# A decode layer pair on one core: more of one pair's values rest in PSUM, and two query weights are loaded into other places

## The chip, the cores and the metric

The kernel runs on one core of a Trainium2 chip. The metric is the device time of one execution in microseconds (us), as a median of several runs. A 95% interval of a ratio is typically 0.13% wide to each side, which is 0.7 us here.

## The reference, cut to what matters

A decoder step for one token, twice over: attention on a cache of 4096 keys and values for each of 32 heads of 192, then a gated feed-forward block of 640 to 1536 to 640. Everything is bf16.

```
x = x + A(layernorm(x))       # q = x wq; softmax(q k^T / sqrt(192)) v; wo
x = x + B(layernorm(x))       # (sigmoid(x wg) * (x wu)) wd
x = x + A(layernorm(x))       # the same weights and the same cache again
x = x + B(layernorm(x))
```

One token means no reuse: each key and value byte enters one product per layer. Heads are handled in 16 pairs. One pair's keys with its Wq, or its values with its Wo, are 3.64 MB; all pairs together are 116 MB. On-chip memory holds seven such units and a smaller region, so the second layer loads nearly all of it again. What is kept from layer 0 to layer 1 is not loaded twice: pairs 0, 14 and 15, the keys of pair 1, and a part of the values of pair 1 in PSUM banks that are free at that time.

## The kernel before: the parts that matter

All loads go through one queue of SyncE, in the order of a list `seq`. A load is issued as soon as what it overwrites has been read, so **a load that must wait holds up every load behind it**. The list at the turn from layer 0 to layer 1 (`MW` are the feed-forward weights in three cuts, `MV` the values of pair 1 in the region where the feed-forward weights lie):

```python
NST = 3 * FW // 2                              # FW = 640
stash = [bank[i][:, 0:NST // 2].bitcast(U32) for i in (3, 6)]
...
MW = {"wg0": (0, 0, 3), ..., "d2": (11, 6, 9), "d3": (14, 9, 12)}     # first cell of the region, from, to
MV = {"v1": (17, len(rc)), "v0": (0, 6), "v2": (6, 11), "v3": (11, 14)}   # cells of FW columns
ST = MV["v3"][1] * FW
VAFTER = {"v0": "u3", "v1": "u1", "v2": "d1", "v3": "d3"}
...
seq += [("wol", 14), ("wol", 15)] + [(k,) for k in (*MW, *MV)] + [("a0", 0), ("wom",), ("a0", 1), ("a0", 2), ("a", 1, 3), ("b", 1, 2)]
...
elif k == "a0":                                # Wq, then keys of pair 2, in three loads
    if f"a14_{it[1]}" not in ev_done:          # over pair 14's Wq and keys: after its Q, after its QK
        return False
    s = A_SLOT[1][2]
    o0, o1 = ((0, WQE), (WQE, A0CUT), (A0CUT, UNIT))[it[1]]
    pg.dma(q_dma(slot(s, o0, o1 - o0), a_in(2, o0, o1)), ...)
```

`("a0", 0)` is the Wq of pair 2. It overwrites pair 14's Wq, so it cannot be issued before layer 1 has computed Q of pair 14 (its queries, the product of x with that Wq). `wom` is Wo of pair 1 (it overwrites pair 1's Wq, so it waits for Q of pair 1). Layer 1 begins with:

```python
mark("a14_0", Q(14, 0))
mark("QM", Q(PM, 1, 5))                        # PM = 1
for i in range(2):                             # values of pair 1: back from PSUM to SBUF
    pg.op("dve", lambda v, i=i: words(v, mreg(ST + i * NST, NST), stash[i]), ...)
ln_sq(xi)
mark("a14_1", QK(14, 0, ks=(0,)))
mark("a14_2", QK(14, 0, ks=(1, 2)))
...
soft(1)
expo(1)
QK(0, 0)
```

## Time and profile before

| | before |
|---|---|
| median of the first 3 runs | 515.14 us (514.93 to 515.77) |
| span of the profiled run | 513.6 us |
| loaded by queue q1 | 218.63 MB |

In the views PE is the matrix engine, PEld its weight loads, DVE VectorE, ACT ScalarE, POOL GpSimd, and SPq the issues of SyncE. The page of the kernel before: the span, busy time by engine, GB/s in 40 slices of 12.8 us, the load queue (packets, MB, share of the 16 DMA engines' span), and the chain that ended last by engine.

```profile
span 513.6 us, 8573 instructions
PE 263.4 (51%) x3716; PEld 137.6 (27%) x3716; DVE 99.2 (19%) x376; ACT 85.2 (17%) x171; POOL 4.2 (1%) x31
...
GB/s 430 425 422 425 426 429 439 451 443 425 429 425 434 426 443 451 435 425 429 411 416 417 410 438 435 433 425 427 453 443 434 434 429 429 426 430 423 426 427 276
...
q1 hardware_dynamic: 9512, 218.63, 99.1%
...
DMA 63%; PE 24%; DVE 7%; ACT 2%; SPq 2%; issue 2%; DVEq 0%; POOL 0%; ACTq 0%; POOLq 0%
```

No engine but the DMA is near its limit. The weakest slices, 20 to 23, are 244 to 295 us, the feed-forward block and the turn into layer 1.

The end of the chain in order of time (start, length, what): the last load lands at 486.16 + 24.89 = 511.05 us.

```profile
486.16 24.89 DMA big<-in_wd_dram
```

The windows view at the turn: window, its length, busy time (and instructions) of PE, PEld, DVE, ACT and POOL, the granted clock, the mean busy share of the DMA engines, GB/s.

```profile
288.00:290.00 2.00, 1.70 (x39) 1.23 (x42) 1.17 (x5) 0.00 (x0) 0.00 (x0) 0.50 1.02 420
290.00:292.00 2.00, 2.00 (x20) 0.55 (x13) 1.03 (x5) 0.00 (x0) 0.00 (x0) 0.50 1.02 406
292.00:294.00 2.00, 1.65 (x29) 1.28 (x29) 1.39 (x2) 0.44 (x2) 0.00 (x0) 0.50 0.96 367
294.00:296.00 2.00, 2.00 (x24) 0.49 (x12) 0.23 (x1) 0.42 (x2) 0.00 (x0) 0.50 1.08 437
```

From 292 to 294 us the stream moves 367 GB/s. The timeline around it: start, length, engine, line. The two SyncE lines are the issues of Wq of pair 2 and Wo of pair 1; line 166 is the copies back from PSUM.

```profile
288.91 0.33 SPq L212 DMA_DIRECT2D big<-in_uc_dram  x1
...
289.31 1.38 SPq L212 DMA_DIRECT2D big<-in_uc_dram  x1
...
289.49 1.34 DVE L166 TENSOR_SCALAR big<-bank 128x480 uint32<-128x480 uint32 x2
290.74 0.15 DVE L361 SCALAR_TENSOR_TENSOR sc<-bank,sc 128x5 f32<-128x5 f32 x1
```

**Measures taken from the packet records of the traces.** The trace has each DMA packet with its time and size; one packet is one row of one load.

- *Outstanding* at an issue: the bytes of all earlier loads minus the bytes moved so far, as time at 428 GB/s, the stream's mean.
- *Packet time* of a load: eight rows per engine, each 7.0 ns plus its size over 27.13 B/ns. This fits the median rows: 102 ns for 2560 B, 149 for 3840, 291 for 7680, 1053 for 28416. The fixed part agrees in kind with the Trainium skill, "DMA: Bandwidth & Descriptors", section "Why small descriptors are slow (HBM only)", which has a fixed overhead per packet.
- *The turn*: from the mark of the last down-projection load `d3` to the mark of pair 3's keys. The mark of a load is the moment when as many bytes have arrived as it and all loads before it hold. It is not the arrival of the load's own last row: the 16 DMA engines run unevenly, and in the kernel before the last row of `d3` came at 286.20 us, 1.1 us after its mark. *Beyond packet times* is the turn's length minus the packet times of its loads.

### The profile page before, as it was taken

To read this page: it belongs to the slowest core of one execution; us is meant where nothing else is said; L and a number is where in the kernel's file an instruction comes from. 1 tells how busy PE (TensorE), PEld (TensorE's weight loads), DVE (VectorE), ACT (ScalarE), POOL (GpSimd) and SP (SyncE) were. 2 spreads that over 40 slices of the span, in tenths; PEclk is the share of its full clock that TensorE was granted. 3 is DMA by queue.
4 is the path that set the end of the run, shared out by engine and by line. 5 is a ranking of instruction groups with operands and counts; after the bars stand their busy time and mean duration, and the time that the engine had idled before them with its cause. 6 is when DMAs were issued, how large, how long until landed. Compare 5 with 4: busy or idle time off the path is not lost.

```text
span 513.6 us, 8573 instructions
## 1 busy us (share of the span) xinstructions
PE 263.4 (51%) x3716; PEld 137.6 (27%) x3716; DVE 99.2 (19%) x376; ACT 85.2 (17%) x171; POOL 4.2 (1%) x31
## 2 busy tenths in 40 slices
PE   0462456344643265345566767864625245634665
PEld 0221222122311132222234434432312122212334
DVE  0221212112211121111121333231202112210311
ACT  0110111011110111011120033130301011101220
POOL 0010000000000000000000000000000000000000
PEclk9955665565566755566575568676857555556655
DMA  9999999999999999999999999999999999999996
GB/s 430 425 422 425 426 429 439 451 443 425 429 425 434 426 443 451 435 425 429 411 416 417 410 438 435 433 425 427 453 443 434 434 429 429 426 430 423 426 427 276
DMA packets 9676, 218.97 MB, mean 426 GB/s; under 512 B 1208, under 2 KB 1208, under 8 KB 4664
## 3 DMA queue, kind: packets, MB, share of 16 engines
q1 hardware_dynamic: 9512, 218.63, 99.1%
q8 instruction: 13, 0.21, 0.1%
q10 hardware_dynamic: 144, 0.06, 0.0%
q14 instruction: 7, 0.06, 0.0%
HBM read 218.69 MB, written 0.00 MB: 426 GB/s over the span
## 4 chain that ended last, share of the span: by engine, by line
DMA 63%; PE 24%; DVE 7%; ACT 2%; SPq 2%; issue 2%; DVEq 0%; POOL 0%; ACTq 0%; POOLq 0%
DMA big<-in_uc_dram 54%; PE scores L410 8%; PE o L467 7%; DMA big<-in_wd_dram 6%; DVE sc L420 3%; DMA big<-in_wu_dram 3%; PE bank L426 2%; SPq L212 2%; PE bank L395 2%; PE bank L502 1%; ACT e_sb L434 1%; PE bank L440 1%; ACT diag L423 1%; DVE sc L452 1%; DVE qs L398 1%
## 5 line engine op out<-in xcount | busy, mean ns | idle before, releaser
L410 PE MATMUL scores<-big,qs 128*32 128x512 bf16 x744 | 81.5, 605 | 9.9 <-DVE qs L398 9.9
L395 PE MATMUL bank<-sh,big 128*128 128x1 bf16 x465 | 17.1, 166 | 133.0 <-DMA big<-in_uc_dram 130.7
L467 PE MATMUL o<-big,et_sb 128*2 128x384 bf16 x1024 | 78.7, 474 | 5.9 <-DMA big<-in_uc_dram 3.4
L423 ACT ACTIVATE diag<-cst,sc 128x128 f32<-128x128 bf16 x32 | 12.8, 402 | 307.5 <-DVE sc L420 299.4
L420 DVE TENSOR_REDUCE sc<-scores 128x1 f32<-128x1024 f32 x31 | 38.0, 1225 | 79.2 <-PE scores L410 79.2
L395 PEld LDWEIGHTS bank<-sh,big 128*128 128x128 bf16 x465 | 14.6, 103 | 136.2 <-DMA big<-in_uc_dram 113.4
L426 PE MATMUL bank<-diag,sc 128*128 128x128 f32 x64 | 22.5, 447 | 47.9 <-ACT diag L423 47.9
L434 ACT ACTIVATE e_sb<-scores,sc 128x1024 bf16<-128x1024 f32 x31 | 37.4, 1205 | 41.8 <-DVE sc L429 39.5
L467 PEld LDWEIGHTS o<-big,et_sb 128*2 128x2 bf16 x1024 | 28.0, 108 | 43.8 <-issue 31.1
L398 DVE TENSOR_TENSOR qs<-bank,cst 128x96 bf16<-128x96 f32 x31 | 8.0, 258 | 162.4 <-PE bank L395 162.4
L410 PEld LDWEIGHTS scores<-big,qs 128*32 128x32 bf16 x744 | 23.7, 131 | 43.0 <-issue 29.6
L426 PEld LDWEIGHTS bank<-diag,sc 128*128 128x128 f32 x64 | 14.1, 274 | 73.0 <-ACT diag L423 71.5
L474 ACT CAST o_sb<-o 128x384 bf16<-128x384 f32 x64 | 29.8, 474 | 22.5 <-PE o L467 22.3
L502 PE MATMUL bank<-sh,big 128*128 128x1 bf16 x480 | 17.2, 165 | 15.2 <-DVE sh L491 14.6
L444 DVE CAST et_sb<-bank 128x64 bf16<-128x64 f32 x32 | 7.2, 225 | 71.8 <-PE bank L440 71.8
L502 PEld LDWEIGHTS bank<-sh,big 128*128 128x128 bf16 x480 | 14.5, 99 | 17.7 <-DVE sh L491 12.1
L427 DVE TENSOR_REDUCE sc<-bank 128x2 f32<-128x128 f32 x32 | 9.3, 292 | 42.1 <-PE bank L426 42.1
L440 PE MATMUL bank<-cst,e_sb 128*128 128x8 bf16 x256 | 11.7, 169 | 6.8 <-ACT e_sb L434 6.7
L440 PEld LDWEIGHTS bank<-cst,e_sb 128*128 128x128 bf16 x256 | 8.9, 101 | 22.9 <-issue 16.4
L450 PE MATMUL o<-sc 128*128 128x2 f32 x62 | 14.0, 295 | 0.6 <-ACT o_sb L474 0.6
L450 PEld LDWEIGHTS o<-sc 128*128 128x128 f32 x62 | 12.1, 243 | 1.9 <-ACT o_sb L474 1.3
L452 DVE RECIPROCAL sc<-o 64x1 f32<-64x1 f32 x62 | 10.2, 164 | 9.5 <-PE o L450 7.8
(76 smaller groups left out, 106.4 us busy)
## 6 DMA issues: line engine op xcount, KB each, us to landing
big<-in_uc_dram SPq DMA_DIRECT2D x20, 7104.0 KB, 22.6
big<-in_uc_dram SPq DMA_DIRECT2D x12, 3552.0 KB, 21.2
big<-in_uc_dram SPq DMA_DIRECT2D x1, 3072.0 KB, 21.5
big<-in_uc_dram SPq DMA_DIRECT2D x4, 768.0 KB, 11.6
big<-in_uc_dram SPq DMA_DIRECT2D x5, 480.0 KB, 6.9
big<-in_uc_dram SPq DMA_DIRECT2D x1, 2048.0 KB, 10.7
big<-in_uc_dram SPq DMA_DIRECT2D x1, 2016.0 KB, 10.6
big<-in_wg_dram SPq DMA_DIRECT2D x4, 480.0 KB, 14.7
```

The source lines that it names most:

```text
L395: ins = t.matmul(qe[:, i:i + 1], lhsT=slot(sa, c * 2 * DH + c0, P), rhs=xq[:, c:c + 1], start=(c == 0), stop=(c == DC - 1))
L410: ins = t.matmul(sc_x[1 + b][32 * j:32 * j + 32, :], lhsT=qs[:, y, k, :], rhs=slot(sa, WQE + k * W + (4 * b + j) * 512, 512), start=(k == ...
L420: pg.op("dve", lambda v: v.reduce_max(out=mx, in_=sc_x[0][:], axis=AX.X), wr=[res("mx")], ex=sc_x[3:5])
L423: pg.op("act", lambda a: a.mul(out=diag[:], in_=ident, mul=mx), rd=[res("cst"), res("mx")], wr=[res("diag")])
L426: pg.op("pe", lambda t: t.matmul(dmx[:, 0:P], lhsT=ones_f, rhs=diag[:], start=True, stop=True), rd=[res("diag"), res("ones")], ex=[rb[2]])
L434: pg.op("act", lambda a: a.activation(out=e_sb[:], in_=sc_x[0][:], func=ACT.Exp, bias=nbias, scale=srs_c, accum_out=rowsum), rd=[res("nbia ...
L440: ins = t.matmul(qe[:, 0:2 * NB].rearrange("p (r x) -> p r x", r=2)[:, :, 4 * b:4 * b + 4], lhsT=e_sb[:, b * P:(b + 1) * P], rhs=sel, star ...
L450: pg.op("pe", lambda t: t.matmul(sm, lhsT=ones_f, rhs=rs2[z], start=True, stop=True), rd=[res(f"rs2{z}"), res("ones")], wr=[res("rsum")], ...
L452: rb[bk].last["dve"] = pg.op("dve", lambda v, h=h: v.reciprocal(out=Rn[z][64 * h:64 * h + 64], in_=sm[64 * h:64 * h + 64, h:h + 1]), rd=[r ...
L467: ins = t.matmul(o8[h][32 * j:32 * j + 2, 0:2 * DH].rearrange("p (a d) -> p a d", a=2), lhsT=et_sb[:, z, h * NB + 2 * u:h * NB + 2 * u + 2 ...
L474: pg.op("act", lambda a, h=h: a.copy(out=o8_sb[:, :, h * DH:(h + 1) * DH], in_=o8[h][:, 0:2 * DH].rearrange("p (a d) -> p a d", a=2)), wr= ...
L502: ins = t.matmul(yT[:, j:j + 1], lhsT=wo[:, c * D + j * P:c * D + (j + 1) * P], rhs=oTb[z][:, c:c + 1], start=False, stop=(c == 2), skip_g ...
```

## The change

It has two parts. First, the third resting place: 507 more fp32 words of each partition, the unused part of bank 7, which else holds only the five columns of the output accumulator. That is 1014 more columns of pair 1's values that layer 1 need not load. Second, the order: the Wq of pair 2 goes into cells of pair 1's values (which must then come back from PSUM later, after that Wq has been used), and the Wq of pair 3 into the place of pair 14's Wq. So the load that must wait for Q of pair 14 is now the Wq of pair 3, and two loads that need not wait stand before it. Q of pair 2 is computed early, kept as three columns, and used when its turn comes.

```diff
-    stash = [bank[i][:, 0:NST // 2].bitcast(U32) for i in (3, 6)]
+    stash = [(bank[i][:, c:c + n].bitcast(U32), 2 * n) for i, c, n in ((3, 0, NST // 2), (6, 0, NST // 2), (7, DC, 512 - DC))]
+    NSV = sum(n for _, n in stash)
 ...
-    MV = {"v1": (17, len(rc)), "v0": (0, 6), "v2": (6, 11), "v3": (11, 14)}
+    MV = {"v1": (17, len(rc)), "v0": (NSV // FW, 6), "v2": (6, 11), "v3": (11, 14), "v4": (14, 17)}
+    VAFTER = {"v1": "u1", "v0": "d1", "v2": "u3", "v3": "d2", "v4": "d3"}
 ...
-    seq += [...] + [(k,) for k in (*MW, *MV)] + [("a0", 0), ("wom",), ("a0", 1), ("a0", 2), ("a", 1, 3), ("b", 1, 2)]
+    seq += [...] + [(k,) for k in (*MW, "v1", "wq2", "v0", "v2", "v3", "v4", "wq3", "wom")] + [("a0", 1), ("a0", 2), ("a", 1, 3), ("b", 1, 2)]
 ...
+        elif k == "wq2":                      # Wq of pair 2, over the first down-projection weights
+            if "done_d0" not in ev_done:
+                return False
+            pg.dma(q_dma(mreg(0, WQE), a_in(2, 0, WQE)), k, wr=rc[0:WQE // FW])
+        elif k == "wq3":                      # Wq of pair 3, over pair 14's
+            if "a14_0" not in ev_done:
+                return False
+            pg.dma(q_dma(slot(A_SLOT[1][2], 0, WQE), a_in(3, 0, WQE)), k, wr=[res(k)], extra=[ev_done["a14_0"]])
 ... # layer 0: a third copy into PSUM, behind the softmax of pair 2
+            if (l, prev) == (0, PM):
+                stow(2, [ev])
 ... # layer 1
             mark("QM", Q(PM, 1, 5))
-            for i in range(2):
-                pg.op("dve", lambda v, i=i: words(v, mreg(ST + i * NST, NST), stash[i]), ...)
             ln_sq(xi)
 ...
-            soft(1)
+            soft(1, hook=lambda: Q(2, None))
+            for i in (2, 0, 1):
+                o, n = sum(m for _, m in stash[:i]), stash[i][1]
+                pg.op("dve", lambda v, i=i, o=o, n=n: words(v, mreg(o, n), stash[i][0]), ..., ex=[rb[7]] if i == 2 else [], own="st")
             expo(1)
```

The loads of the turn, in queue order, with the bytes of one row:

```
before: v1 2816 | v0 7680 | v2 6400 | v3 3840 | Wq2* 3840 | Wo1* 3840 | keys2* 8192, 16384 | Wq3+keys3* 28416
after:  v1 2816 | Wq2 3840 | v0 1812 | v2 6400 | v3 3840 | v4 3840 | Wq3* 3840 | Wo1* 3840 | keys2* 8192, 16384 | keys3* 24576
(* waits for PE's work of layer 1)
```

More of the change, by code (lines that the diff above doesn't have):

```diff
@@ L51, in __init__, with op @@
         self.seg = None
-    def op(self, eng, fn, rd=(), wr=(), ex=(), multi=False, own=None):
+    def op(self, eng, fn, rd=(), wr=(), ex=(), multi=False, own=None, after=()):
         d = {}
@@ L70, in op @@
                     add(ev)
+        for ev in after:
+            add(ev)
         if eng == "pe":
@@ L129, in decode_kernel @@
     et_sb = sb("et_sb", [P, 2, 2 * NB], BF16)
-    sc = sb("sc", [P, 27 + 5 * DC + 2 * FC], FP32)
+    sc = sb("sc", [P, 30 + 5 * DC + 2 * FC], FP32)
+    q2 = sc[:, 27 + 5 * DC + 2 * FC:30 + 5 * DC + 2 * FC]
     tick = sc[0:1, 24 + 5 * DC + 2 * FC:25 + 5 * DC + 2 * FC]
@@ L181, in decode_kernel @@
     MAFTER = {"d0": ("wg0",), "d1": ("wg1",), "u2": ("wg2",), "u3": ("wg3",), "d2": ("wg3", "u0"), "d3": ("u1",)}
-    MV = {"v1": (17, len(rc)), "v0": (0, 6), "v2": (6, 11), "v3": (11, 14)}
-    VAFTER = {"v1": "u1", "v0": "d1", "v2": "u3", "v3": "d2"}
-    ST = MV["v3"][1] * FW
-    VAFTER = {"v0": "u3", "v1": "u1", "v2": "d1", "v3": "d3"}
+    MV = {"v1": (17, len(rc)), "v0": (NSV // FW, 6), "v2": (6, 11), "v3": (11, 14), "v4": (14, 17)}
+    VAFTER = {"v1": "u1", "v0": "d1", "v2": "u3", "v3": "d2", "v4": "d3"}
     PLACE = {s: i for i, s in enumerate((0, 3, 2, 1, 4, 5, 6))}
@@ L227, in decode_kernel @@
     seq = [("a", 0, 0)] + [("c", 0, p) for p in range(1, 15)] + [("a", 0, 15), ("b", 0, 14)] + last_values(0, 15)
-    seq += [("wol", 14), ("wol", 15)] + [(k,) for k in (*MW, *MV)] + [("a0", 0), ("wom",), ("a0", 1), ("a0", 2), ("a", 1, 3), ("b", 1, 2)]
+    seq += [("wol", 14), ("wol", 15)] + [(k,) for k in (*MW, "v1", "wq2", "v0", "v2", "v3", "v4", "wq3", "wom")] + [("a0", 1), ("a0", 2), ("a", 1, 3), ("b", 1, 2)]
     seq += [("b", 1, 3), ("a", 1, 4), ("b", 1, 4), ("a", 1, 5), ("a", 1, 6), ("b", 1, 5)]
@@ L265, in try_load @@
                 return False
-            pg.dma(q_dma(slot(s, 0, UNIT), a_in(it[2])), f"c{it[1]}{it[2] % 2}" if it[1:] in ((0, 15), (1, 4), (1, 5), (1, 6), (1, 13)) else f"a{it[1]}_{it[2]}", wr=[rslot[s]])
+            o0 = WQE if it[1:] == (1, 3) else 0
+            pg.dma(q_dma(slot(s, o0, UNIT - o0), a_in(it[2], o0)), f"c{it[1]}{it[2] % 2}" if it[1:] in ((0, 15), (1, 4), (1, 5), (1, 6), (1, 13)) else f"a{it[1]}_{it[2]}", wr=[rslot[s]])
         elif k == "b":
@@ L290, in try_load @@
             s = A_SLOT[1][2]
-            o0, o1 = ((0, WQE), (WQE, A0CUT), (A0CUT, UNIT))[it[1]]
+            o0, o1 = ((WQE, A0CUT), (A0CUT, UNIT))[it[1] - 1]
             pg.dma(q_dma(slot(s, o0, o1 - o0), a_in(2, o0, o1)), f"a0{it[1]}", wr=[res(f"a0{it[1]}")] + ([rslot[s]] if it[1] == 2 else []),
@@ L307, in try_load @@
             c0, c1 = MV[k]
-            o0, o1 = c0 * FW, min(c1 * FW, ME)
+            o0, o1 = max(c0 * FW, NSV), min(c1 * FW, ME)
             pg.dma(q_dma(mreg(o0, o1 - o0), b_in(PM, o0, o1)), k, wr=rc[c0:-(-o1 // FW)])
+        elif k == "wq2":
[6 more added lines that the diff above has]
+            pg.dma(q_dma(slot(A_SLOT[1][2], 0, WQE), a_in(3, 0, WQE)), k, wr=[res(k)], extra=[ev_done["a14_0"]])
         elif k == "wom":
@@ L390, in Q @@
             sa = A_SLOT[l][p]
+            w, rw = slot(sa, 0, WQE), [rslot[sa]]
+            if (l, p) == (1, 2):
+                w, rw = mreg(0, WQE), rc[0:WQE // FW]
+            elif (l, p) == (1, 3):
+                s2 = A_SLOT[l][2]
+                w, rw = slot(s2, 0, WQE), [rslot[s2], res("wq3")]
             def f(t):
@@ L394, in f @@
                     for c in range(DC):
-                        ins = t.matmul(qe[:, i:i + 1], lhsT=slot(sa, c * 2 * DH + c0, P), rhs=xq[:, c:c + 1], start=(c == 0), stop=(c == DC - 1))
+                        ins = t.matmul(qe[:, i:i + 1], lhsT=w[:, c * 2 * DH + c0:c * 2 * DH + c0 + P], rhs=xq[:, c:c + 1], start=(c == 0), stop=(c == DC - 1))
                 return ins
-            ev = pg.op("pe", f, rd=[res("xq"), rslot[sa]] + ([res("a00")] if l == 1 and p == 2 else []), ex=[rb[bk]])
+            ev = pg.op("pe", f, rd=[res("xq")] + rw, ex=[rb[bk]])
+            if y is None:
+                pg.op("dve", lambda v: v.tensor_copy(out=q2, in_=qe[:, 0:3]), wr=[res("q2")], ex=[rb[bk]])
+                return ev
             pg.op("dve", lambda v: v.tensor_tensor(out=qs[:, y], in0=qe[:, 0:3].unsqueeze(2).to_broadcast([P, 3, 32]), in1=mask3, op=ALU.mult),
@@ L412, in f @@
                 return ins
-            ev = pg.op("pe", f, rd=[res(f"qs{y}"), rslot[sa]] + ([res("a00"), res("a01"), res("a02")] if l == 1 and p == 2 else []), ex=sc_x[3:5])
+            ev = pg.op("pe", f, rd=[res(f"qs{y}"), rslot[sa]] + ([res("a01"), res("a02")] if l == 1 and p == 2 else []), ex=sc_x[3:5])
             if ks[-1] == 2 and not (l == 0 and ("a", p) in KEPT) and not (l == 1 and p in (PM, 14)):
@@ L522, in PVn @@
                 release(sv)
+            return ev
         def scale_pm():
@@ L526, in scale_pm, with stow @@
                   rd=[res("cst"), res("srs")], wr=[res("pm_s")])
+        def stow(i, after=()):
+            sv, o = B_SLOT[0][PM], sum(n for _, n in stash[:i])
+            ev = pg.op("dve", lambda v: words(v, stash[i][0], slot(sv, v_at(PM) + o, stash[i][1])), rd=[rval[sv]], wr=[res(f"stash{i}")], own="st", after=after)
+            rslot[sv].rd.append(ev)
         def step(p, prev):
             if l == 0 and prev > 0:
-                PVn(prev - 1, 1 - prev % 2)
+                ev = PVn(prev - 1, 1 - prev % 2)
             Q(p, 0)
@@ L553, in loop @@
                     if (l, p) == (0, PM):
-                        sv = B_SLOT[0][PM]
-                        for i in range(2):
-                            ev = pg.op("dve", lambda v, i=i: words(v, stash[i], slot(sv, v_at(PM) + ST + i * NST, NST)), rd=[rval[sv]], wr=[res(f"stash{i}")], own="st")
-                            rslot[sv].rd.append(ev)
+                        stow(0)
+                        stow(1)
             pg.seg = None
@@ L577, in attention @@
             mark("QM", Q(PM, 1, 5))
-            for i in range(2):
-                pg.op("dve", lambda v, i=i: words(v, mreg(ST + i * NST, NST), stash[i]), rd=[res(f"stash{i}")], wr=rc[ST // FW:ST // FW + 3], own="st")
             ln_sq(xi)
@@ L589, in attention @@
             Q(0, 0)
-            soft(1)
+            soft(1, hook=lambda: Q(2, None))
+            for i in (2, 0, 1):
+                o, n = sum(m for _, m in stash[:i]), stash[i][1]
+                pg.op("dve", lambda v, i=i, o=o, n=n: words(v, mreg(o, n), stash[i][0]), rd=[res(f"stash{i}")], wr=rc[o // FW:-(-(o + n) // FW)],
+                      ex=[rb[7]] if i == 2 else [], own="st")
             expo(1)
@@ L604, in attention @@
             ET(1)
-            Q(2, 0)
+            pg.op("dve", lambda v: v.tensor_tensor(out=qs[:, 0], in0=q2.unsqueeze(2).to_broadcast([P, 3, 32]), in1=mask3, op=ALU.mult),
+                  rd=[res("cst"), res("q2")], wr=[res("qs0")])
             packed(2, 0, PM)
```

## The prediction

> **What bounds the kernel.** The load stream. The queue table gives q1 99.1% of the 16 DMA engines' span, 218.63 MB; the chain of waits is 63% DMA and ends in a weight load (486.16 to 511.09 us). PE is busy 51%, VectorE 19%. The last loads, from 482.9 us on, are issued far ahead (by the packet records 4 us of data is outstanding at the first, 22 us at the last), so the end moves with the stream, and compute counts only where it lets the stream run dry.
>
> Where does it? I added up, from the packet records, bytes issued minus bytes moved at each issue. The low point is the turn into layer 1, with small loads that wait for PE: 2.4 us is outstanding when the Wq of pair 2 is issued (288.91 us, after Q of pair 14). The next issue, Wo of pair 1, took 1.38 us instead of 0.33, while the two 0.65 us copies from PSUM ran on VectorE (289.5 to 290.8). In the windows view 292 to 294 us moves only 367 GB/s. The four loads from pair 2's Wq to its keys end about 0.6 us later than their packet times explain.
>
> **What changes, costed.**
> 1. Bytes: the values resting in PSUM grow from 1920 to 2934 columns; 1014 x 2 B x 128 = 0.26 MB less is loaded. At 430 GB/s: -0.60 us.
> 2. Rows: the packet records give 102 ns for 2560 B, 149 for 3840, 291 for 7680: about 7 ns each plus size over 27.1 B/ns. One 7680 B load shrinks to 1812 B (75 ns, an estimate from that fit), one 3840 B load is added, pair 3's load is cut into 3840 and 24576 B: +0.1 us. The Trainium skill, "DMA: Bandwidth & Descriptors", section "Why small descriptors are slow (HBM only)", tells of a fixed overhead per packet; this trace agrees, at about 7 ns. Net of 1 and 2: -0.5 us.
> 3. Order: two loads that need not wait for Q of pair 14 now stand before it in the queue: pair 2's Wq and a values load. At 288.9 us about 3.0 us should be outstanding, and the copies from PSUM move to 303.4 us, away from the issues. The bubble should mostly close: -0.5 us.
> 4. VectorE: a third copy in and out, 507 words, about 0.69 us each. The copy in falls in layer 0, where VectorE idles over 2 us; free. The three copies out take 2.0 us after the second softmax (303.4 us); the next VectorE work that matters starts at 305.59. They just fit.
> 5. PE: Q of pair 2 moves 20 us earlier, into an idle stretch. Off the path.
>
> **Critical part.** About 1.0 us, all of it the stream's.
>
> **Prediction.** 514.1 us, 513.4 to 514.9. Faster by over 2%: 0.005; within 2%: 0.985; slower by over 2%: 0.01.
>
> **What would show it.** q1 moves 218.37 MB. The Wo issue takes 0.33 us; no window between 288 and 300 us falls much below 400 GB/s; the last load ends about 1 us earlier. The copies out end before the maximum over pair 0's scores starts, and the load that follows it (values of pair 2) is issued by 305.6 us.
>
> **What would make it wrong.** The unaligned 1812 B rows cost more than the fit; the bubble merely moves; the copies slow another load's issue, or delay VectorE enough to starve the stream near 306 us, where 4.4 us is outstanding (3.4 after the change).

## The result

| | before | after |
|---|---|---|
| median, 6 runs each | 515.03 us (514.58 to 515.87) | 514.15 us (513.96 to 514.55) |
| ratio, 95% interval | | 0.9981 (0.9968 to 0.9994) |
| span of the profiled run | 513.6 us | 512.7 us |

A ratio is the mean time of one kernel's fast runs over that of the other's of the same rounds, so it is not quite the ratio of the two medians. By the rule of 2% the verdict is "same"; the interval does exclude no change. Two later pairs of 5 runs against 9 gave 514.26 against 515.11 (0.9976, 0.9961 to 0.9992) and, on another chip, 514.64 against 514.79 (0.9995, 0.9982 to 1.0009). So the gain is between 0.15 and 0.9 us by the medians of three sessions. The prediction's 514.1 us and its range hold. That it fits to 0.05 us is luck: the changed kernel's own median was 514.15, 514.26 and 514.64 us in the three sessions.

The page of the changed kernel, the same parts:

```profile
span 512.7 us, 8581 instructions
PE 263.9 (51%) x3716; PEld 138.7 (27%) x3716; DVE 100.3 (20%) x379; ACT 85.0 (17%) x171; POOL 4.2 (1%) x31
...
GB/s 431 426 423 426 427 430 428 430 461 439 426 430 426 435 430 426 443 457 430 394 420 415 419 438 441 434 425 425 461 439 435 426 426 430 445 426 417 427 429 273
...
q1 hardware_dynamic: 9800, 218.37, 99.1%
```

The bytes fell by 0.26 MB, and the packets rose by 288: there are two more loads (`v4`, and the Wq of pair 3 apart from its keys) of 128 rows, and each load brings 16 small completion packets, 2 x (128 + 16). The queue is as full as before: 99.1%.

The chain's end: the last load lands at 485.35 + 24.70 = 510.05 us, 1.00 us earlier.

```profile
485.35 24.70 DMA big<-in_wd_dram
```

The windows at the turn: none falls below 410 GB/s.

```profile
288.00:290.00 2.00, 1.72 (x38) 1.23 (x42) 0.98 (x7) 0.00 (x0) 0.00 (x0) 0.50 1.03 416
290.00:292.00 2.00, 2.00 (x23) 0.63 (x16) 0.00 (x0) 0.00 (x0) 0.00 (x0) 0.50 1.00 410
292.00:294.00 2.00, 1.65 (x25) 1.20 (x29) 1.40 (x3) 0.51 (x3) 0.00 (x0) 0.50 1.04 425
294.00:296.00 2.00, 2.00 (x20) 0.49 (x12) 0.21 (x1) 0.34 (x1) 0.00 (x0) 0.50 1.05 440
```

The timeline: the issue of Wo of pair 1, then the three copies out of PSUM (line 170), the maximum over pair 0's scores that must not be delayed (line 440), and the load that its scores release.

```profile
289.23 0.97 SPq L214 DMA_DIRECT2D big<-in_uc_dram  x1
...
303.25 1.94 DVE L170 TENSOR_SCALAR big<-bank 128x507 uint32<-128x507 uint32 x3
305.51 1.23 DVE L440 TENSOR_REDUCE sc<-scores 128x1 f32<-128x1024 f32 x1 [0.32 <-PE scores L430]
...
305.50 0.33 SPq L214 DMA_DIRECT2D big<-in_uc_dram  x1
```

The copies end at 305.19, 0.3 us before the maximum starts, and that waits for PE as before. The load is issued at 305.50, with 3.7 us outstanding (3.4 predicted). All this is about as predicted. One thing is not as predicted: the issue of Wo still takes 0.97 us although no copy runs on VectorE between 289 and 303 us. The predicted cause of the long issue can't be right for this kernel.

Where the microsecond came from, by packet records of one execution of each kernel:

| stretch of the stream | before | after | difference |
|---|---|---|---|
| mark of `d3` | 285.10 | 285.22 | +0.12 |
| the turn (`d3` to pair 3's keys) | 25.33 | 24.45 | **-0.88** |
| of it packet times | 24.51 | 24.02 | -0.49 |
| of it beyond packet times | 0.82 | 0.43 | -0.39 |
| mark of pair 3's keys to the landing of the last load | 200.62 | 200.38 | -0.24 |

The loads of this last stretch are the same in all twelve traces, and it took 199.6 to 201.2 us in them. So 0.24 us there is within its spread, and the landing of the last load in one execution can be off by as much as the effects that are sought.

### The profile page after: what moved, and what is told of

It is laid out like the page before. It is cut to its first block, busy times and chain, and to the rows that moved or that the text cites. A ratio compares the mean times of both kernels' runs of the same rounds, so it can differ in the third digit from the quotient of the medians.

```text
span 512.7 us, 8581 instructions
## 1 busy us (share of the span) xinstructions
PE 263.9 (51%) x3716; PEld 138.7 (27%) x3716; DVE 100.3 (20%) x379; ACT 85.0 (17%) x171; POOL 4.2 (1%) x31
## 3 DMA queue, kind: packets, MB, share of 16 engines
q1 hardware_dynamic: 9800, 218.37, 99.1%
## 4 chain that ended last, share of the span: by engine, by line
DMA 63%; PE 24%; DVE 7%; ACT 3%; SPq 2%; issue 2%; DVEq 0%; POOL 0%; ACTq 0%; POOLq 0%
DMA big<-in_uc_dram 54%; PE scores L430 8%; PE o L487 7%; DMA big<-in_wd_dram 6%; DMA big<-in_wu_dram 3%; DVE sc L440 3%; PE bank L446 2%; SPq L214 2%; PE bank L412 2%; ACT e_sb L454 2%; PE bank L522 1%; PE bank L460 1%; ACT diag L443 1%; DVE sc L472 1%; DVE qs L418 1%
## 5 line engine op out<-in xcount | busy, mean ns | idle before, releaser
L430 PE MATMUL scores<-big,qs 128*32 128x512 bf16 x744 | 82.9, 613 | 10.3 <-DVE qs L418 9.6
```

The lines of the kernel that those rows point to most:

```text
L430: ins = t.matmul(sc_x[1 + b][32 * j:32 * j + 32, :], lhsT=qs[:, y, k, :], rhs=slot(sa, WQE + k * W + (4 * b + j) * 512, 512), start=(k == ...
```

## The experiments

**Theory A**: the gain has two halves that need each other. Fewer bytes save packet time, and the new order keeps enough loads outstanding over the point where the queue must wait for Q of pair 14. **Rival B**: the copies on VectorE held the issue of Wo and made the dry spell. **Rival C**: only the bytes count. Two more rivals (D, and E against F) came up on the way.

Ten runs were made, in three sessions; with the two kernels themselves that gives twelve traces. All results were correct.

### 1. The copies alone moved (x3_copies_late)

```diff
             mark("QM", Q(PM, 1, 5))
-            for i in range(2):
-                pg.op("dve", ... words(v, mreg(ST + i * NST, NST), stash[i]), ...)
 ...
             soft(1)
+            for i in range(2):
+                pg.op("dve", ... words(v, mreg(ST + i * NST, NST), stash[i]), ...)
             expo(1)
```

> The kernel before with one edit: its two copies from PSUM back to SBUF move from just after the three first queries of layer 1 (289.5 us) to behind the second softmax (about 303.4 us). Bytes and order of the loads stay. Theory A (the stream runs thin because loads stand behind a query in the queue): the copies are innocent, the issue of pair 1's Wo still takes about 1 us or more, the last weight load ends within 0.1 us of the kernel before (511.05 us). Rival B (the copies on VectorE hold that issue): the issue takes 0.33 us, and the last load ends about 0.4 us earlier.

Measured: 514.81 us against 515.11 (ratio 0.9988, 0.9973 to 1.0004: unclear). The timeline of this run: the issue of Wo, and what VectorE does first after the queries.

```profile
289.41 1.28 SPq L212 DMA_DIRECT2D big<-in_uc_dram  x1
...
289.59 0.15 DVE L361 SCALAR_TENSOR_TENSOR sc<-bank,sc 128x5 f32<-128x5 f32 x1
```

The issue took 1.28 us with no copy in sight: rival B falls as the cause of the long issue. The last load landed at 510.83 us, 0.2 us before the kernel before's: neither the 0.1 us of A nor the 0.4 us of B. The turn was 25.10 us, 0.59 beyond packet times, so a little shorter than the 25.33 before. That is not the copies' doing as far as the issue goes: 2.66 us was outstanding here when Q of pair 14 ended, against 2.38. The stream and PE stand a few tenths of a microsecond differently to each other in each execution; experiment 4 shows that the loss goes with what is outstanding.

### 2. The bytes alone (x1_bytes_only)

Experiment 1 plus the third resting place, old order. The columns are taken from `v0`, whose rows shrink from 7680 to 5652 B.

```diff
-    stash = [bank[i][:, 0:NST // 2].bitcast(U32) for i in (3, 6)]
+    stash = [bank[i][:, 0:NST // 2].bitcast(U32) for i in (3, 6)] + [bank[7][:, DC:512].bitcast(U32)]
+    N7 = 2 * (512 - DC)
 ...
-            o0, o1 = c0 * FW, min(c1 * FW, ME)
+            o0, o1 = c0 * FW or N7, min(c1 * FW, ME)
 ... # and the third copy in and out, at the places of the changed kernel
```

> The last experiment plus the third resting place (0.26 MB less is loaded, the 7680 B rows become 5652 B), with the old order of the loads. Packet times alone: -0.60 us. Theory A: less is outstanding (about 1.8 us instead of 2.4) when the Wq of pair 2 is issued at 288.9 us, so a part of the saving is given back as idle time of the DMA engines; the last load ends 0.0 to 0.4 us earlier than without the smaller load. Rival C (only the bytes count, the turn never runs dry): the full 0.6 us earlier, 510.45 us.

Measured: 514.66 us against 515.11 for the kernel before and 514.81 for experiment 1 (ratio to before 0.9986, 0.9970 to 1.0002: unclear). The turn took **25.33 us, as before the change**: 0.6 us less packet time, 1.42 us beyond it instead of 0.82. Windows view of this run:

```profile
290.00:292.00 2.00, 2.00 (x20) 0.55 (x12) 0.00 (x0) 0.00 (x0) 0.00 (x0) 0.50 1.02 351
292.00:294.00 2.00, 1.65 (x29) 1.25 (x29) 1.37 (x2) 0.40 (x2) 0.00 (x0) 0.50 1.01 361
294.00:296.00 2.00, 2.00 (x24) 0.52 (x16) 0.25 (x2) 0.46 (x2) 0.00 (x0) 0.50 0.96 389
```

Three windows run at 351 to 389 GB/s where the changed kernel has 410 to 440. Against its own control (experiment 1, turn 25.10) the smaller load bought nothing in the turn. The readout named beforehand says otherwise: the last load landed at 510.16 us, 0.7 us before experiment 1's, which is what rival C forecast. But this profiled run was the fastest of its five (514.07), and of that 0.7 us none arose in the turn: the stream was 0.3 us earlier before it, and 0.6 us shorter in the 200 us behind it, with identical loads. (Those 200 us were 1.0 us shorter than the kernel before's.) So its span and its landing must not be read as the effect of the bytes. Rival C falls by the turn, one trace against one; the times alone would not have told.

### 3. The order alone (x2_order_only)

The changed kernel with two resting places; `v0` has rows of 3840 B.

```diff
-    stash = [... ((3, 0, NST // 2), (6, 0, NST // 2), (7, DC, 512 - DC))]
+    stash = [... ((3, 0, NST // 2), (6, 0, NST // 2))]
 ...
-            if (l, prev) == (0, PM):
-                stow(2, [ev])
 ...
-            for i in (2, 0, 1):
+            for i in (0, 1):
```

> The changed kernel without the third resting place: 0.26 MB more in rows of 3840 B, but the new order. Packet times alone against the kernel before: +0.1 us. Theory A: about 3.7 us is outstanding when Q of pair 14 ends, no dry spell, the 0.4 us of idle engines is saved: last load ends at about 510.75 us, 0.3 us before the kernel before and 0.7 after the changed one. Rival C (only the bytes count): last load at 511.1 us or later, no gain at all.

Measured: 514.97 us against 515.11 (0.9989, 0.9973 to 1.0004: unclear). The turn took 24.99 us, with 0.36 beyond packet times, which is as low as any: the order alone leaves no dry spell, as A says. How much shorter this makes the turn depends on the execution of the old order that it is held against: 0.34 us against the kernel before, 0.11 against experiment 1, 0.07 against x8 below, which all load the same bytes. No window from 286 to 302 us falls below 407 GB/s; those that were the weakest before:

```profile
290.00:292.00 2.00, 2.00 (x20) 0.85 (x24) 0.47 (x4) 0.00 (x0) 0.00 (x0) 0.50 1.00 407
292.00:294.00 2.00, 1.65 (x29) 0.88 (x25) 0.75 (x2) 0.01 (x1) 0.00 (x0) 0.76 1.03 421
```

3.1 us was outstanding, less than the 3.7 expected, because the issues of this run came 0.7 us later than in the changed kernel. The profiled run was the slowest of its five (515.47), and its last load landed at 511.46 instead of the expected 510.75; the excess arose in the last 40 us of the stream, where all kernels load the same. The expectation for the landing thus failed, and the one that no dry spell would be left held.

> The changed kernel once more, beside the three others, as the yardstick of this chip: about 0.9 us faster than the kernel before, last load ends at about 510.1 us, and the issue of pair 1's Wo takes about 1 us although no copy runs then.

The yardstick of the same chip: 514.26 us; turn 24.49 us, 0.46 beyond packet times; the issue of Wo took 0.96 us; last load at 510.50 us, not the 510.1 expected.

### 4. Dose and response: one or two loads put behind the waiting one (x6_gate_one_early, x5_gate_two_early)

If what stands before the waiting load is the point, putting the waiting load further forward must cost time in proportion. Bytes and rows are those of the changed kernel.

```diff
-"v1", "wq2", "v0", "v2", "v3", "v4", "wq3", "wom"
+"v1", "wq2", "v0", "v2", "v3", "wq3", "v4", "wom"     # x6
+"v1", "wq2", "v0", "v2", "wq3", "v3", "v4", "wom"     # x5
```

> The same with pair 3's Wq ahead of one values load. About 2.0 to 2.2 us is outstanding when Q of pair 14 ends. Theory A: 1.1 to 1.25 us beyond packet times in the turn, 0.7 us more than the changed kernel. Rival D: no change.

> The changed kernel with pair 3's Wq, which waits for Q of pair 14, placed ahead of two values loads instead of behind them; same bytes, same rows. The four kernels so far lie on one curve: of the time between the end of the last down-projection load and the end of pair 3's keys, the part beyond packet times is 0.4 us as long as about 2.9 us or more is outstanding when that query ends, and grows by 1 us for each us less (2.7 us: 0.6; 2.4: 0.8; 1.85: 1.4). Here about 1.0 us is outstanding. Theory A: 2.3 us beyond packet times, the last load ends about 1.9 us later than in the changed kernel. Rival D (the gain of the new order is not from what stands before the query): no change beyond 0.3 us.

Measured: 514.88 us for x6 and 516.08 us for x5, against 514.93 for the kernel before on that chip. x5 is slower than the kernel before by 1.0024 (1.0010 to 1.0038), although it loads 0.26 MB less; x6 is level with it (1.0001, 0.9988 to 1.0015). Turn: 25.59 us for x6 and 26.89 for x5, so 1.1 and 2.4 us above the changed kernel. The last load of x5 landed at 512.32 us, 2.3 us later than in the changed kernel (1.9 expected). Rival D falls. The windows view of x5:

```profile
288.00:290.00 2.00, 1.70 (x39) 1.29 (x43) 0.98 (x7) 0.00 (x0) 0.00 (x0) 0.50 0.80 323
290.00:292.00 2.00, 2.00 (x23) 0.55 (x12) 0.00 (x0) 0.00 (x0) 0.00 (x0) 0.50 0.92 293
292.00:294.00 2.00, 1.65 (x29) 1.20 (x29) 1.31 (x2) 0.34 (x2) 0.00 (x0) 0.50 0.99 255
```

PE, VectorE and ACT are busy as before, and the stream moves 255 to 323 GB/s. Note the DMA share of 0.99 in the last row: a busy share near 1 does not mean full rate. The rows in flight in that window took 1.5 times their packet time on average.

All kernels on one curve (from the packet records; outstanding is taken at the issue of the first load that waits for Q of pair 14):

| kernel | outstanding, us | turn beyond packet times, us | turn, us |
|---|---|---|---|
| x5, two loads behind | 0.74 | 2.87 | 26.89 |
| x1, bytes only | 1.85 | 1.42 | 25.33 |
| x6, one load behind | 1.87 | 1.57 | 25.59 |
| before | 2.38 | 0.82 | 25.33 |
| x3, copies late | 2.66 | 0.59 | 25.10 |
| x7 again | 2.78 | 0.69 | 24.50 |
| x8, fetch moved | 2.84 | 0.56 | 25.06 |
| after again | 2.95 | 0.46 | 24.49 |
| after, third time | 2.97 | 0.42 | 24.44 |
| x7, more at rest | 3.00 | 0.54 | 24.34 |
| x2, order only | 3.09 | 0.36 | 24.99 |
| after | 3.16 | 0.43 | 24.45 |

Each row is one execution. Above about 2.9 us the loss is flat at 0.36 to 0.54. Below it grows with each us that is missing: from 2.9 to 2.38 by about 0.4, from there to 1.86 (mean of x1 and x6) by 0.7, and to 0.74 by 1.4, so by 0.7 to 1.3 us per us. The slope was expected to be 1, and x5 and x6 came out 0.3 to 0.6 us worse than said.

### 5. What held the issue of Wo (x8_fetch_moved)

In six traces the issue of Wo ended 0.36 to 0.37 us after a 16384 B packet of queue q8, which is of the kind "instruction", had ended (for the kernel before: packet 289.39 to 290.31, issue 289.31 to 290.69). The Trainium skill, "Runtime: NRT & Kernel Launch", section "Instruction fetch mechanics", says that an engine's instructions come in blocks of 16 KiB, 256 instructions, over a DMA queue of its sequencer. To move the packet, 36 matmuls that change no result were put into two gaps of PE, on the kernel before:

```diff
                 mark("done_" + k, proj(0, range(f0, f1), g_of, 0, rc[c:c + f1 - f0]))
+                if k in ("wg0", "wg1"):
+                    def idle(t):
+                        for _ in range(18):
+                            ins = t.matmul(bank[2][:, 255:256], lhsT=ident, rhs=xm[:, 0, 0:1], start=True, stop=True)
+                        return ins
+                    pg.op("pe", idle, rd=[res("cst"), res("xm0")], ex=[rb[2]])
```

> The kernel before with 36 idle matmuls in two gaps in which PE waits for gate weights; they change no result and move PE's fetches of instructions to an earlier time. In all six traces the issue of pair 1's Wo ended 0.36 to 0.37 us after a 16 KB instruction packet of queue q8 did. Theory E (that packet holds the issue, and with it a part of the dry spell): with the packet elsewhere the issue takes 0.33 us and less than 0.82 us is lost in the turn, about 0.5. Rival F (a coincidence): the issue still takes 0.8 us or more, and the turn still loses 0.8.

Measured: 514.76 us against 514.93 (0.9996, 0.9983 to 1.0010). The packet came at 286.05 to 287.01 instead of 289.4, so it is PE's. The issue of Wo (first line) fell to 0.41 us. And another issue, which takes 0.33 us in the kernel before, now was long (second line; the third down-projection load):

```profile
289.52 0.41 SPq L212 DMA_DIRECT2D big<-in_uc_dram  x1
...
278.74 0.88 SPq L212 DMA_DIRECT2D big<-in_wd_dram  x1
```

A q8 packet had moved there too, to 278.32 to 279.25; the issue ended 0.38 us after it. Theory E holds for the issue. In all twelve traces there are 14 places where the second of two loads issued within 0.7 us of each other falls into such a packet. In each, the second issue ended 0.36 to 0.38 us after the packet, whatever it loaded: in x5 and x6 it is a values load, not Wo. A first or single issue during such a packet took its usual 0.33 us. Why the first goes through and the second does not, no run shows. Nor is a fetch the only thing that makes an issue long: in the row of loads issued without a wait from 258 us on, the kernel before has issues of 2.01 us (at 262.39) and 1.56 us (at 264.45) with no q8 packet during them, and every other trace has two such issues there. That cause stays open.

For the time, E's forecast was met (0.56 us lost in the turn, about 0.5 expected), but this doesn't prove it: x8 also had more outstanding, 2.84 us against 2.38, and its 0.56 lies on the curve between kernels that had the long issue (x3: 0.59 at 2.66; after again: 0.46 at 2.95). So no separate cost of the long issue can be seen; one of 0.1 us would be lost in the scatter of the curve.

### 6. More of the same (x7_more_rest, x7_again, after_third)

376 more columns at rest: the first two banks filled, and 124 free words of the bank of the queries.

```diff
-((3, 0, NST // 2), (6, 0, NST // 2), (7, DC, 512 - DC))
+((3, 0, 512), (6, 0, 512), (7, DC, 512 - DC), (2, 260, 124))
 ... # and a fourth copy in and out, held apart from PE's use of bank 2
```

> The changed kernel with 376 more columns of pair 1's values at rest: the two first banks filled to 512 words, and 124 free words of the bank of the queries. 0.096 MB less is loaded, the 1812 B rows become 1060 B. Theory A: what is outstanding at Q of pair 14 falls from about 3.1 to 2.8 us, just at the knee, so 0.15 to 0.25 us is gained over the changed kernel, hardly more than its noise. Rival: past the knee already, nothing gained.

> The version with 376 more columns at rest once more, now beside the changed kernel on one chip. If the 0.1 us by which the turn was shorter is all there is, its median is 0.0 to 0.3 us below the changed kernel's, within the spread of the runs.

> The changed kernel beside it: about 0.9 us faster than the kernel before; the turn takes 24.5 us, 0.4 to 0.5 us of it beyond packet times.

Measured: 513.84 us against 514.93 (0.9980) in the first pass, on one chip; in the second, beside the changed kernel, 514.40 against 514.64, and 514.79 for the kernel before. There the forecast that the changed kernel would be 0.9 us faster failed (0.15), while the one for its turn held. The means of the five runs in that last pass are 514.49 and 514.50, which is no difference. The turn was 24.34 and 24.50 us, with 0.54 and 0.69 beyond packet times, at 3.00 and 2.78 us outstanding. Packet times are 0.22 us shorter than in the changed kernel, and most of that went back. This fits the theory: past this point, bytes saved before the waiting load are bytes missing in front of it. So no version was found that is clearly better than the changed kernel.

## Why the prediction was right, and where it was not

1. **The bound** (the load stream; the end moves with the stream): right. The turn became 0.88 us shorter, the 200 us behind it 0.24 us, which is within the spread of that stretch, and the last load landed 1.00 us earlier.
2. **Bytes and rows, -0.5 us net**: right, -0.49 us in packet times. The unaligned 1812 B rows took 75 ns, as the fit said.
3. **Order, -0.5 us**: right in mechanism, too large: -0.39 us beyond packet times in the two first traces, and -0.22 us if the three traces with the old order and all its bytes (0.82, 0.59, 0.56) are held against the three of the changed kernel (0.43, 0.46, 0.42). The runs add what the prediction did not say: its items 2 and 3 do not add up freely. The bytes without the order shortened the turn by nothing (x1), the order without the bytes by 0.07 to 0.34 us (x2), both by 0.6 to 0.9, each according to which execution of the old order it is held against. The bytes are worth their packet time only because the order keeps the queue filled.
4. **"The Wo issue takes 0.33 us"**: wrong. It took 0.97. The step that failed was to see the copies on VectorE at the same time as the long issue and take the one for the other's cause. x3 moved the copies and the issue stayed long; x8 moved an instruction packet of PE and it became short. For the total this did not matter, because the dry spell does not hang on that issue.
5. **VectorE just fits**: right, with 1.94 us for three copies (2.0 predicted) and 0.3 us to spare. The copy into PSUM in layer 0 took 0.68 us, as estimated, and delayed nothing.
6. **2.4 us outstanding before, 3.0 after**: right, with 2.38, and 3.16, 2.95 and 2.97. There is one trace of the kernel before. x3 and x8 load the same and had 2.66 and 2.84, so a part of the 0.82 us beyond packet times in the kernel before, on which the prediction built its item 3, is the luck of that execution. This may be why the gain ranges from 0.15 to 0.9 us over the sessions; that was not tested.

What stays open: the 0.36 to 0.54 us beyond packet times that no order removed, and why as much as 2.9 us must be outstanding.

## What to carry to other kernels

In a kernel bound by one in-order load queue, look for the load that waits for compute and ask what stands before it: work out the bytes outstanding at its issue, and keep them above what the machine needs (about 2.9 us here). Saving bytes in front of such a load gained nothing in the turn while the queue ran dry there (x1); put loads that need not wait in front, and then save bytes. When a long issue or a slow window coincides with some other engine's work, move that work before blaming it.

## What the Trainium skill lacked or had wrong

- "DMA: Bandwidth & Descriptors", section "Specifications", gives 0.6 us to the first byte for loads issued from SyncE. It doesn't say from when this counts. Here the first packet on the empty queue started 1.01 us after the start of the first issue, which takes 0.39 us itself, so 0.62 us after its end: counted from there the figure agrees. No page says how much must be outstanding when an issue waits for compute: the runs show a loss below 2.9 us, of 0.7 to 1.3 us per us, with waiting loads of 0.5 to 3.6 MB.
- The same page, section "Why small descriptors are slow (HBM only)", describes a fixed overhead per packet but has no time for rows of some KB. The runs fit about 7 ns per row and engine: by their median times on 16 engines 387 GB/s for 1812 B rows (75 ns), 412 for 3840 B (149 ns), 433 for 56832 B (2098 ns).
- "Runtime: NRT & Kernel Launch", section "Instruction fetch mechanics", calls the cost of crossing a 16 KiB boundary "mostly hidden". No page says that one engine's fetch can hold another's DMA issue: in 14 of 14 places the second of two close issues of SyncE ended 0.36 to 0.38 us after PE's 16 KiB packet, and took up to 1.38 us instead of 0.33. No run shows a cost of it in the kernel's time.
